# A two-layer SiLU kernel: the order of its first loads, the place of a table load, and a first tile taken in two halves

## The chip, the cores and the metric

The kernel runs on one core of one Trainium2 chip. A core has five engines that work side by side: TensorE (matmuls and transposes), VectorE and ScalarE (elementwise work), GpSimd, and SyncE, which here only issues transfers. ScalarE issues some transfers too. Each of the two has a queue of its own, and both queues are served by the core's 16 DMA engines. The metric is device time in microseconds (us), less is better. Times are the median of several runs; the profile is one execution.

## The reference

x has 2048 rows and 640 columns, w1 is 640 x 1728, w2 is 1728 x 640, all in bf16. The result is `silu(x @ w1) @ w2`, with silu(h) = h * sigmoid(h):

```python
h = jnp.einsum("bsd,df->bsf", x, w1)
h = _silu(h)
out = jnp.einsum("bsf,fd->bsd", h, w2)
```

## The kernel before

**Tiles.** The 640 columns of x, over which the first product is summed, are cut into 5 contraction tiles of 128 (`dt` 0 to 4). The 1728 columns of w1 are 13 tiles of 128 and a half one (`ft`). The 2048 rows are four chunks of 512 (`sc`). The first product is made transposed: a matmul holds a 128 x 128 tile of w1 as its weights and streams 512 columns of x transposed (`xT_sb`) past it, and its result, h transposed, is summed over the five contraction tiles in one of the 8 banks of PSUM (`ps`). ScalarE then takes the sigmoid and VectorE multiplies (lines 197 and 200). The second product (line 319) follows when all of h is there.

**Order.** The program is a list of operations written out by hand: `add` (used throughout) appends an operation with the engine it runs on and the operations it depends on, and each engine runs its own operations strictly in the order of the list, waiting on semaphores where an operation depends on another engine or on a transfer. The order of the calls is thus the order on each engine and in each transfer queue. No planner moves anything.

**The loads at the start.** The first chunk of x comes as it lies in memory (`x0_sb`, helper `load_x0`, line 144) and is transposed by TensorE; the other chunks come through transposing transfers (line 235), which wait for the first of the two late pieces of w1. The transfers of the first chunk are: contraction tile 0 in two halves of rows of 64 KB (`x0_a` on SyncE, `x0_b` on ScalarE), tiles 1 and 2 of 128 KB each (`x0_c`, `x0_d`, ScalarE), and tiles 3 and 4 together, 256 KB (`x0_e`, ScalarE). The first 6 column tiles of w1 come by contraction tile, 192 KB each (`w1_0` to `w1_4`, helper `load_w1`, line 148), all on SyncE; the last two of them wait for `x0_a` and `x0_b`. The other columns of w1 follow in two large pieces. On ScalarE a small sigmoid on a scratch tile (line 155) comes after its four transfers; it has no use but to load the sigmoid's table early (the row ACT_TABLE_LOAD).

**TensorE's start.** TensorE first runs five warm-up matmuls of 512 columns and one of 256 on constants (`warm_up`, line 164). Then it transposes tile 0 of x, four blocks of 128 x 128, into PSUM in two halves, and VectorE copies each half to `xT_sb` (line 178). Two more warm-up matmuls follow, of 512 and 256 columns. Then `column_group` (line 258) runs the first 6 column tiles of w1 for the first chunk: the outer loop goes over the five contraction tiles, the inner one over the 6 column tiles, each with its own bank. The first matmul of each contraction tile waits for that tile of x transposed and for that tile of w1. After the second matmul of a contraction tile, `transpose_next` puts in the four transposes of the next tile of x; VectorE copies the even tiles out (line 178), ScalarE the odd ones (line 180). The remaining column tiles go through `unit` (line 213), all five contraction tiles of one bank in a row.

In what follows, "x's tile n" is contraction tile n of the first chunk of x, and "w1's tile n" is contraction tile n of w1's first six column tiles.

Of the kernel before, what the change touches and what calls it, by code (L numbers as in the profile page):

```python
# [20 lines left out]
class Plan:  # L21
# [9 lines left out]
    def add(self, eng, emit, deps=(), group=None):  # L31
        op = Op(eng, emit, [d for d in deps if d is not None], group)
        self.ops.append(op)
        return op
# [40 lines left out]
def bass_standalone__dense_activation_silu__prompt_kernel(  # L75
# [13 lines left out]
    P = 128  # L89
    H = P // 2  # L90
    SCH = 512
    DT = D // P
# [5 lines left out]
    JB = SCH // P  # L98
# [4 lines left out]
    with ExitStack() as es:  # L103
        def sb(name, shape, dtype):
            return es.enter_context(nc.sbuf_tensor(name, shape, dtype))

        xT_sb = sb("xT_sb", [P, DT, S], bf16)
        w1_sb = sb("w1_sb", [P, DT, F], bf16)
# [9 lines left out]
        ps = es.enter_context(nc.psum_tensor("ps", [P, NBANK, SCH], fp32))  # L118
# [6 lines left out]
        add = plan.add  # L125
        bank_free = [[] for _ in range(NBANK)]
        turn = [0]

        def take_bank():
            b = turn[0] % NBANK  # L130
            turn[0] += 1
            return b


        FA = 6
# [7 lines left out]
        def load_x0(eng, name, j0, j1, d0, d1):  # L143
            return add(eng, lambda e: e.dma_start(
                out=x0_sb[:, j0:j1, d0 * P:d1 * P], in_=x0_v[:, j0:j1, d0 * P:d1 * P]), group=name)

        def load_w1(eng, name, d0, d1, f0, f1, deps=()):
            return add(eng, lambda e: e.dma_start(
                out=w1_sb[:, d0:d1, f0:f1], in_=w1_v[:, d0:d1, f0:f1]), deps, group=name)

        x0_a = [load_x0("sp", "x0_a", 0, JB // 2, 0, 1), load_x0("act", "x0_b", JB // 2, JB, 0, 1)]
        w1_lo = [load_w1("sp", "w1_0", 0, 1, 0, FA * P)]
        x0_c = [load_x0("act", "x0_c", 0, JB, 1, 2), load_x0("act", "x0_d", 0, JB, 2, 3), load_x0("act", "x0_e", 0, JB, 3, DT)]
        w1_lo += [load_w1("sp", f"w1_{dt}", dt, dt + 1, 0, FA * P) for dt in (1, 2)]
        add("act", lambda e: e.activation(out=warm_sb[:, :], in_=warm_sb[:, :], func=ACT.Sigmoid), [warm])  # L155
        w1_lo += [load_w1("sp", f"w1_{dt}", dt, dt + 1, 0, FA * P, x0_a) for dt in (3, 4)]
        w1_dma = [load_w1("sp", f"w1_{name}", 0, DT, w1_cuts[g] * P, min(w1_cuts[g + 1] * P, F))
                  for g, name in enumerate("ab")]
# [3 lines left out]
        def warm_up(columns):  # L162
            for n in columns:
                add("pe", lambda e, n=n: e.matmul(  # L164
                    ps[:, NBANK - 1, 0:n], lhsT=ones[:, 0:P], rhs=ones[:, 0:n], start=True, stop=True))
# [3 lines left out]
        def transpose_x0(dt, j0, j1, b):  # L169

            dst = ps[:, b, :].bitcast(bf16)[:, j0 * P:j1 * P]
            out = xT_sb[:, dt, j0 * P:j1 * P]
            for j in range(j0, j1):
                t = add("pe", lambda e, j=j: e.transpose(  # L174
                    dst[:, (j - j0) * P:(j - j0 + 1) * P], x0_sb[:, j, dt * P:(dt + 1) * P], ident[:, :]),
                    [x0_a[j // (JB // 2)], id_b] if dt == 0 else [x0_c[min(dt, 3) - 1]] + bank_free[b])
            if dt % 2 == 0:
                c = add("dve", lambda e: e.tensor_copy(out=out, in_=dst), [t])  # L178
            else:
                c = add("act", lambda e: e.copy(out=out, in_=dst), [t])  # L180
            bank_free[b] = [c]
            return c

        def x_deps(sc, c0, n):
            return x0T if sc == 0 else x1_of if sc == 1 else [x_dma[sc]]

        def w1_deps(ft):
            return [w1_dma[max(g for g in range(len(w1_dma)) if w1_cuts[g] <= ft)]] if ft >= FA else w1_lo
# [5 lines left out]
        def silu(b, parts, n, pe):  # L194
            s = sig_turn[0] % NSIG
            sig_turn[0] += 1
            a = add("act", lambda e: e.activation(  # L197
                out=sig_sb[:, s, 0:n], in_=ps[:, b, 0:n], func=ACT.Sigmoid), [pe, sig_free[s]])
            for rows, ft, cols in parts:
                v = add("dve", lambda e, rows=rows, ft=ft, cols=cols: e.tensor_tensor(  # L200
                    out=hT_sb[rows, ft, cols], in0=ps[rows, b, 0:n], in1=sig_sb[rows, s, 0:n],
                    op=ALU.mult), [a])
                chunk_done[cols.start // SCH] = v
                if ft == FR:
                    tail_done[cols.start // SCH] = v
            bank_free[b] = [v]
            sig_free[s] = v

        def unit(sc, ft, c0, n):
            b = take_bank()  # L210
            cols = slice(sc * SCH + c0, sc * SCH + c0 + n)
            for dt in range(DT):
                pe = add("pe", lambda e, dt=dt: e.matmul(  # L213
                    ps[:, b, 0:n], lhsT=w1_sb[:, dt, ft * P:(ft + 1) * P], rhs=xT_sb[:, dt, cols],
                    start=(dt == 0), stop=(dt == DT - 1)),
                    x_deps(sc, c0, n) + w1_deps(ft) + bank_free[b] if dt == 0 else ())
            silu(b, [(slice(0, P), ft, cols)], n, pe)

        def tail_unit(sc):
            b = take_bank()  # L220
            for dt in range(DT):
                for hh in range(2):
                    pe = add("pe", lambda e, dt=dt, hh=hh: e.matmul(  # L223
                        ps[hh * H:(hh + 1) * H, b, :], lhsT=w1_sb[:, dt, FR * P:F],
                        rhs=xT_sb[:, dt, (sc + hh) * SCH:(sc + hh + 1) * SCH],
                        start=(dt == 0), stop=(dt == DT - 1), skip_group_check=True),
                        x_deps(sc, 0, SCH) + x_deps(sc + 1, 0, SCH) + w1_deps(FR) + bank_free[b]
                        if dt == 0 else ())
            silu(b, [(slice(hh * H, (hh + 1) * H), FR, slice((sc + hh) * SCH, (sc + hh + 1) * SCH))
                     for hh in range(2)], SCH, pe)  # L230

        x_dma, x1_of, w2_dma = {}, [], []
        for sc in range(1, NSC):
# [7 lines left out]
            if sc == 2:  # L241
                half = FR // 2
# [6 lines left out]

        def column_group(sc, x_dep, w1_dep, between=None):  # L250

            banks = [take_bank() for _ in range(FA)]
            for dt in range(DT):
                for ft in range(FA):
                    deps = bank_free[banks[ft]] if dt == 0 else []
                    if ft == 0:
                        deps = deps + [x_dep[dt], w1_dep[dt]]
                    pe = add("pe", lambda e, dt=dt, ft=ft: e.matmul(  # L258
                        ps[:, banks[ft], :], lhsT=w1_sb[:, dt, ft * P:(ft + 1) * P],
                        rhs=xT_sb[:, dt, sc * SCH:(sc + 1) * SCH],  # L260
                        start=(dt == 0), stop=(dt == DT - 1)), deps)
                    if dt == DT - 1:
                        silu(banks[ft], [(slice(0, P), ft, slice(sc * SCH, (sc + 1) * SCH))], SCH, pe)
                    if between and ft == 1:
                        between(dt + 1)

        def transpose_next(dt):
            if dt < DT:
                x0T.append(transpose_x0(dt, 0, JB, FA + dt % 2))

        half = [transpose_x0(0, k * JB // 2, (k + 1) * JB // 2, FA - 2 + k) for k in range(2)]
        x0T = [half[1]]
        warm_up([SCH, 2 * P])
        column_group(0, x0T, w1_lo, transpose_next)
        for ft in range(FA, FR):
            unit(0, ft, 0, SCH)

        for sc in range(1, NSC):
            if sc == 1:
                column_group(sc, x1_of, w1_lo)  # L280
            for ft in range(FA if sc == 1 else 0, FR):
                unit(sc, ft, 0, SCH)
        reg_done = dict(chunk_done)
# [111 lines left out]
```

## Time and profile before

| what | value |
|---|---|
| median of 3 runs | 126.33 us (125.98 to 126.65) |
| the profiled execution | 126.5 us, its span 125.2 us |
| TensorE busy | 122.1 us, 98% of the span |
| first instruction of TensorE | at 0.77 us |
| first matmul of the column group (L258) | at 4.37 us |
| first matmul of `unit` (L213) | at 12.36 us |
| ACT_TABLE_LOAD (L155) | 1283 ns, from 2.91 us |

The span runs from the first to the last instruction; the execution's own time holds 1.3 us more. In the views, L258 is a line of the kernel before. A group of instructions stands as start, duration, engine, line, operation, the tile written and the tiles read, and how often. PE is TensorE's matmul, PEld its weight load, DVE is VectorE, ACT ScalarE, SPq and ACTq the transfer queues of SyncE and ScalarE. The chain is the sequence of work that ended last, followed back from the end of the execution; "issue" in it is time in which an engine waited for nothing that the profile shows. In the table of stretches each row has the stretch, its length, the busy time of PE, PEld, DVE, ACT and POOL (with the number of instructions that begin), the granted clock, the busy share of the DMA engines and GB/s. A transfer's row ends with its size in KB and the time from its issue to the landing of its last part.

### The profile page before, as it was taken

To read this page: it belongs to the slowest core of one execution; us is meant where nothing else is said; L and a number is where in the kernel's file an instruction comes from. 1 tells how busy PE (TensorE), PEld (TensorE's weight loads), DVE (VectorE), ACT (ScalarE), POOL (GpSimd) and SP (SyncE) were. 2 spreads that over 40 slices of the span, in tenths; PEclk is the share of its full clock that TensorE was granted. 3 is DMA by queue.
4 is the path that set the end of the run, shared out by engine and by line. 5 is a ranking of instruction groups with operands and counts; after the bars stand their busy time and mean duration, and the time that the engine had idled before them with its cause. 6 is when DMAs were issued, how large, how long until landed. Compare 5 with 4: busy or idle time off the path is not lost.

```text
span 125.2 us, 2101 instructions
## 1 busy us (share of the span) xinstructions
PE 122.1 (98%) x902; PEld 57.4 (46%) x902; DVE 45.6 (36%) x72; ACT 39.4 (32%) x69; POOL 0.7 (1%) x6
## 2 busy tenths in 40 slices
PE   7999999999999999999999999999999999999992
PEld 2544444444444444444444444444444444445481
DVE  0112986069766666666673020202020120202022
ACT  0523953087555555555540010101010110101021
POOL 2000000000000000000000000000000000000000
PEclk9999999999999999999999999999999999999999
DMA  3995355589910000000000001114120200112424
GB/s 77 314 385 181 86 113 72 112 237 390 276 43 0 5 0 0 3 0 0 0 0 5 0 0 31 26 22 168 52 105 5 105 0 21 26 21 73 157 98 117
DMA packets 19625, 10.41 MB, mean 83 GB/s; under 512 B 13344, under 2 KB 19616, under 8 KB 19616
## 3 DMA queue, kind: packets, MB, share of 16 engines
q1 hardware_dynamic: 17472, 9.56, 26.6%
q10 hardware_dynamic: 2144, 0.72, 2.2%
q8 instruction: 7, 0.11, 0.4%
q14 instruction: 2, 0.02, 0.1%
HBM read 5.16 MB, written 2.62 MB: 62 GB/s over the span
## 4 chain that ended last, share of the span: by engine, by line
PE 98%; DVE 0%; issue 0%
PE ps L319 47%; PE ps L213 34%; PE ps L258 11%; PE ps L164 3%; PE ps L223 2%; PE ps L174 1%; DVE o_sb L330 0%
## 5 line engine op out<-in xcount | busy, mean ns | idle before, releaser
L319 PE MATMUL ps<-w_sb,hT_sb 64*128 64x512 bf16 (+2 forms) x486 | 47.3, 352 | 0.0
L200 DVE TENSOR_TENSOR hT_sb<-ps,sig_sb 128x512 bf16<-128x512 f32 (+1 forms) x56 | 37.0, 688 | 19.0 <-ACT sig_sb L197 18.9
L213 PE MATMUL ps<-xT_sb,w_sb 128*128 128x512 bf16 x200 | 43.5, 379 | 0.0
L197 ACT ACTIVATE sig_sb<-ps 128x512 bf16<-128x512 f32 x54 | 30.7, 606 | 24.9 <-PE ps L213 16.4
L319 PEld LDWEIGHTS ps<-w_sb,hT_sb 64*128 64x128 bf16 x486 | 23.3, 94 | 23.7
L213 PEld LDWEIGHTS ps<-xT_sb,w_sb 128*128 128x128 bf16 x200 | 19.6, 98 | 23.6
L330 DVE CAST o_sb<-ps 128x512 bf16<-128x512 f32 (+2 forms) x9 | 5.7, 632 | 37.6 <-PE ps L319 37.6
L332 ACT CAST o_sb<-ps 128x512 bf16<-128x512 f32 (+2 forms) x9 | 4.8, 538 | 38.6 <-PE ps L319 38.6
L258 PE MATMUL ps<-xT_sb,w_sb 128*128 128x512 bf16 x60 | 14.4, 387 | 0.0
L319 PE MATMUL ps<-hT_sb,w_sb 64*128 64x512 bf16 x108 | 12.3, 376 | 0.0
L258 PEld LDWEIGHTS ps<-xT_sb,w_sb 128*128 128x128 bf16 x60 | 5.6, 99 | 6.7 <-DVE xT_sb L178 0.7
L319 PEld LDWEIGHTS ps<-hT_sb,w_sb 64*128 64x128 bf16 x108 | 5.2, 94 | 6.6 <-issue 0.4
L330 DVE CAST oT_sb<-ps 128x512 bf16<-128x512 f32 x2 | 1.4, 692 | 11.7 <-PE ps L319 11.7
L332 ACT CAST oT_sb<-ps 128x512 bf16<-128x512 f32 x2 | 1.2, 586 | 13.6 <-PE ps L319 13.6
L178 DVE COPY xT_sb<-ps 128x256 bf16<-128x256 bf16 (+1 forms) x4 | 1.4, 358 | 8.6 <-PE ps L174 8.6
L164 PE MATMUL ps<-const-bfloat16-1.0 128*128 128x512 bf16 (+1 forms) x8 | 3.3, 572 | 0.8 <-PEq L380 0.8
L174 PEld LDWEIGHTS ps<-ident,x_sb 128*128 128x128 bf16 x20 | 1.9, 115 | 1.7 <-DMA x_sb<-in_x_dram 0.7
L174 PE MATMUL ps<-ident,x_sb 128*128 128x128 bf16 x20 | 2.4, 256 | 0.0
L180 ACT COPY xT_sb<-ps 128x512 bf16<-128x512 bf16 x2 | 1.2, 585 | 3.9 <-PE ps L174 3.9
L223 PE MATMUL ps<-xT_sb,w_sb 128*64 128x512 bf16 x20 | 2.3, 381 | 0.0
L155 ACT ACT_TABLE_LOAD x1 | 1.3, 1283 | 2.9 <-issue 2.9
L164 PEld LDWEIGHTS ps<-const-bfloat16-1.0 128*128 128x128 bf16 x8 | 1.0, 137 | 1.9 <-issue 1.9
(9 smaller groups left out, 2.3 us busy)
## 6 DMA issues: line engine op xcount, KB each, us to landing
out_dram<-o_sb SPq DMA_DIRECT2D x14, 160.0 KB, 1.9
w_sb<-in_w_dram SPq DMA_DIRECT2D x1, 1120.0 KB, 7.6
w_sb<-in_w_dram SPq DMA_DIRECT2D x5, 192.0 KB, 4.8
w_sb<-in_w_dram SPq DMA_DIRECT2D x1, 960.0 KB, 5.3
w_sb<-in_w_dram SPq DMA_DIRECT2D x1, 640.0 KB, 6.3
w_sb<-in_w_dram SPq DMA_DIRECT2D x1, 560.0 KB, 7.3
x_sb<-in_x_dram ACTq DMA_DIRECT2D x2, 128.0 KB, 3.8
x_sb<-in_x_dram ACTq DMA_DIRECT2D x1, 256.0 KB, 5.8
```

The source lines that it names most:

```text
L155: add("act", lambda e: e.activation(out=warm_sb[:, :], in_=warm_sb[:, :], func=ACT.Sigmoid), [warm])
L164: add("pe", lambda e, n=n: e.matmul(ps[:, NBANK - 1, 0:n], lhsT=ones[:, 0:P], rhs=ones[:, 0:n], start=True, stop=True))
L174: t = add("pe", lambda e, j=j: e.transpose(dst[:, (j - j0) * P:(j - j0 + 1) * P], x0_sb[:, j, dt * P:(dt + 1) * P], ident[:, :]), [x0_a[j ...
L178: c = add("dve", lambda e: e.tensor_copy(out=out, in_=dst), [t])
L197: a = add("act", lambda e: e.activation(out=sig_sb[:, s, 0:n], in_=ps[:, b, 0:n], func=ACT.Sigmoid), [pe, sig_free[s]])
L200: v = add("dve", lambda e, rows=rows, ft=ft, cols=cols: e.tensor_tensor(out=hT_sb[rows, ft, cols], in0=ps[rows, b, 0:n], in1=sig_sb[rows, ...
L213: pe = add("pe", lambda e, dt=dt: e.matmul(ps[:, b, 0:n], lhsT=w1_sb[:, dt, ft * P:(ft + 1) * P], rhs=xT_sb[:, dt, cols], start=(dt == 0), ...
L223: pe = add("pe", lambda e, dt=dt, hh=hh: e.matmul(ps[hh * H:(hh + 1) * H, b, :], lhsT=w1_sb[:, dt, FR * P:F], rhs=xT_sb[:, dt, (sc + hh) * ...
L258: pe = add("pe", lambda e, dt=dt, ft=ft: e.matmul(ps[:, banks[ft], :], lhsT=w1_sb[:, dt, ft * P:(ft + 1) * P], rhs=xT_sb[:, dt, sc * SCH:( ...
L319: pe = add("pe", lambda e, b=b, n=n, lhsT=lhsT, rhs=rhs, ft=ft: e.matmul(ps[:, b, 0:n], lhsT=lhsT, rhs=rhs, start=(swap == 0 and ft == 0), ...
L330: ev = add("dve", lambda e, b=b, n=n, dst=dst: e.tensor_copy(out=dst, in_=ps[:, b, 0:n]), [pe])
L332: ev = add("act", lambda e, b=b, n=n, dst=dst: e.copy(out=dst, in_=ps[:, b, 0:n]), [pe])
```

## The change

Three things are done.

1. In the list of transfers, x's tiles 1 and 2 go from ScalarE's queue to SyncE's, directly behind w1's tile 0. SyncE's order becomes: half of x's tile 0, w1's tile 0, x's tiles 1 and 2, w1's tile 2, then w1's tiles 3 and 4 and the rest as before.
2. ScalarE's order becomes: the other half of x's tile 0, the table load with the small sigmoid, w1's tile 1 (which was SyncE's), and x's tiles 3 and 4.
3. `column_group` can take a contraction tile in parts of rows. For the first chunk's tile 0 it has two: the first 256 rows of x for all 6 column tiles, then the other 256, so 12 matmuls of 256 columns in place of 6 of 512. The first of each part waits only for that half's copy. The next tile's transposes come after the fourth of these matmuls. The other tiles, and the second chunk's group, have one part as before. The warm-up matmul of 512 columns after the first transposes is taken out; the one of 256 stays.

```diff
         x0_a = [load_x0("sp", "x0_a", 0, JB // 2, 0, 1), load_x0("act", "x0_b", JB // 2, JB, 0, 1)]
         w1_lo = [load_w1("sp", "w1_0", 0, 1, 0, FA * P)]
-        x0_c = [load_x0("act", "x0_c", 0, JB, 1, 2), load_x0("act", "x0_d", 0, JB, 2, 3), load_x0("act", "x0_e", 0, JB, 3, DT)]
-        w1_lo += [load_w1("sp", f"w1_{dt}", dt, dt + 1, 0, FA * P) for dt in (1, 2)]
+        x0_c = [load_x0("sp", "x0_c", 0, JB, 1, 2), load_x0("sp", "x0_d", 0, JB, 2, 3)]
         add("act", lambda e: e.activation(out=warm_sb[:, :], in_=warm_sb[:, :], func=ACT.Sigmoid), [warm])
+        w1_lo += [load_w1("act", "w1_1", 1, 2, 0, FA * P), load_w1("sp", "w1_2", 2, 3, 0, FA * P)]
+        x0_c += [load_x0("act", "x0_e", 0, JB, 3, DT)]
...
-            return x0T if sc == 0 else x1_of if sc == 1 else [x_dma[sc]]
+            return x0T[-1] if sc == 0 else x1_of if sc == 1 else [x_dma[sc]]
...
             banks = [take_bank() for _ in range(FA)]
             for dt in range(DT):
-                for ft in range(FA):
-                    deps = bank_free[banks[ft]] if dt == 0 else []
-                    if ft == 0:
-                        deps = deps + [x_dep[dt], w1_dep[dt]]
-                    pe = add("pe", lambda e, dt=dt, ft=ft: e.matmul(
-                        ps[:, banks[ft], :], lhsT=w1_sb[:, dt, ft * P:(ft + 1) * P],
-                        rhs=xT_sb[:, dt, sc * SCH:(sc + 1) * SCH],
-                        start=(dt == 0), stop=(dt == DT - 1)), deps)
-                    if dt == DT - 1:
-                        silu(banks[ft], [(slice(0, P), ft, slice(sc * SCH, (sc + 1) * SCH))], SCH, pe)
-                    if between and ft == 1:
-                        between(dt + 1)
+                parts = len(x_dep[dt])
+                for h in range(parts):
+                    c0, c1 = h * (SCH // parts), (h + 1) * (SCH // parts)
+                    for ft in range(FA):
+                        deps = [x_dep[dt][h], w1_dep[dt]] if ft == 0 else []
+                        if dt == 0 and h == 0:
+                            deps = deps + bank_free[banks[ft]]
+                        pe = add("pe", lambda e, dt=dt, ft=ft, h=h, c0=c0, c1=c1: e.matmul(
+                            ps[:, banks[ft], c0:c1], lhsT=w1_sb[:, dt, ft * P:(ft + 1) * P],
+                            rhs=xT_sb[:, dt, sc * SCH + c0:sc * SCH + c1],
+                            start=(dt == 0 and h == 0), stop=(dt == DT - 1), skip_group_check=True), deps)
+                        if dt == DT - 1:
+                            silu(banks[ft], [(slice(0, P), ft, slice(sc * SCH, (sc + 1) * SCH))], SCH, pe)
+                        if between and h == 0 and ft == 2 * parts - 1:
+                            between(dt + 1)
...
-                x0T.append(transpose_x0(dt, 0, JB, FA + dt % 2))
+                x0T.append([transpose_x0(dt, 0, JB, FA + dt % 2)])
...
-        x0T = [half[1]]
-        warm_up([SCH, 2 * P])
+        x0T = [half]
+        warm_up([2 * P])
...
-                column_group(sc, x1_of, w1_lo)
+                column_group(sc, [[d] for d in x1_of], w1_lo)
```

In the changed kernel the lines after the loads stand a little lower: the column group's matmul is L264, the transposes L175, the warm-ups L165, `unit` L214.

## The prediction

> **What bounds the kernel now.** I read the page first, for the chain that ended last.
>
> ```profile
> PE 98%; DVE 0%; issue 0%
> PE ps L319 47%; PE ps L213 34%; PE ps L258 11%; PE ps L164 3%; PE ps L223 2%; PE ps L174 1%; DVE o_sb L330 0%
> ```
>
> TensorE is the whole chain, and the last line says where a change of the loading order can act at all: in the warm-up matmuls (L164), the transposes (L174) and the first column group (L258). From L213 on nothing is touched, and TensorE never stands there. So I read the start of the chain in order of time, which has one break: "issue" ahead of 4.37 us, the first real matmul.
>
> ```profile
> 3.28 0.43 PE ps L174 x4
> 3.70 0.64 PE ps L164 x2
> 4.34 0.03 issue
> 4.37 1.01 PE ps L258 x2
> 5.38 0.43 PE ps L174 x4
> 5.80 1.30 PE ps L258 x6
> ```
>
> What ends that break? The timeline names VectorE, but the same timeline shows its two copies done at 3.53 + 0.51 = 4.04.
>
> ```profile
> 3.53 0.51 DVE L178 COPY xT_sb<-ps 128x256 bf16<-128x256 bf16 x2 [2.63 <-PE ps L174]
> 4.34 0.14 PEld L258 LDWEIGHTS ps<-xT_sb,w_sb 128*128 128x128 bf16 x2 [0.69 <-DVE xT_sb L178]
> ```
>
> The wait is for two things, and the other is w1's tile 0. The DMA view around its issue (1.25 us) gives the time to its landing:
>
> ```profile
> w_sb<-in_w_dram SPq DMA_DIRECT2D x1, 192.0 KB, 3.0
> x_sb<-in_x_dram ACTq DMA_DIRECT2D x1, 128.0 KB, 3.3
> ```
>
> So w1's tile 0 lands at 1.25 + 3.0 = 4.25, and the matmul follows 0.12 us later, at 4.37. The second row is x's tile 1, issued by ScalarE at almost the same instant (1.26). The table of stretches shows that the two compete: the DMA engines are full from 2 us on.
>
> ```profile
> 2.00:3.00 1.00, 1.00 (x4) 0.33 (x3) 0.00 (x0) 0.09 (x1) 0.00 (x0) 1.00 0.99 203
> 3.00:4.00 1.00, 1.00 (x8) 0.64 (x6) 0.47 (x2) 1.00 (x1) 0.00 (x0) 1.00 1.08 282
> 4.00:5.00 1.00, 0.97 (x4) 0.28 (x3) 0.03 (x1) 0.42 (x2) 0.00 (x0) 1.00 1.05 297
> ```
>
> The last two columns are the DMA share and GB/s. After the first matmul every tile comes before its turn: the tightest is x's tiles 3 and 4, issued at 2.35, landing 5.8 us later at 8.15, with the transposes that read them at 8.46 right behind the matmul before them.
>
> **The pace of TensorE.** Weight loads of the first 512-column warm-ups start 0.43 us apart (1.15, 1.58, 2.01, 2.43), while ten L258 matmuls from 10.37 take 2.16 us, 0.216 each. The matmul starting at 5.60 still takes 0.43 us by itself, those after 5.86 take 0.38, and early ones 0.63: the pace doubles at about 5.70, 4.93 us after the first matmul at 0.77. The page's granted clock does not show it (9 in every slice). So a start moved from 4.37 to 4.37 - d wins not d but d x (1 - 0.216/0.427) = 0.495 d, as long as the doubling stays at 5.70: the time won is spent at half pace.
>
> **The change, part by part.**
>
> *x's tiles 1 and 2 move from ScalarE's queue to SyncE's, behind w1's tile 0.* w1's tile 0 keeps its place (third issue of all, at 1.25) but loses its competitor. Bounds for its landing: 4.25, as now; or what the bytes ahead of it need if it is served alone. x's two first halves and w1's tile 0 are 320 KiB, 328 kB. The finer table of stretches moved 8 kB up to 2.0, 187 GB/s to 2.5, 219 GB/s to 3.0 and 277 GB/s to 3.5: 211 kB by 3.0, the other 117 kB by 3.42. From the last byte to landing: the two half tiles (131 kB) are through at 2.64 by the same count and land at 0.75 + 2.3 = 3.05, so 0.41; w1's tile 0 lands at 3.83. I take this end, since its nearest row, the two half tiles with nothing behind them, is that situation. TensorE starts 0.12 later: about 3.96, d = 0.41.
>
> *The first contraction tile by halves of rows; the 512-column warm-up goes.* TensorE now ends its warm-ups at 4.14 (transposes to 3.50, then 768 columns at half pace); without the 512 it is free at 3.71. The first matmul needs only the first copy, done at 3.53 + 0.29 = 3.82, not 4.04. So neither holds 3.96, and without these two parts the start would be 4.14. The price: 12 matmuls of 256 columns for 6 of 512, the same columns. Six run at half pace, 0.213 each; six at full pace, where 256 columns are half of 0.216, and weight loads (97 ns) hide behind them as they do now behind 128-column transposes that start 0.056 apart. A price per matmul could be 0 to 0.05 (the transposes'); I take 0, because the transposes carry twice as many loads per column without a gap. That is 0 to 0.3 us in the range. The transposes of tile 1 come after four half matmuls, as many columns as now after two.
>
> *What the moved transfers then meet.* From 3.96: four half matmuls to 4.81, transposes to 5.24, two halves to 5.67, six at full pace to 6.33, tile 1. SyncE's issues are about 0.5 apart, so x's tile 1 goes at 1.75 and tile 2 at 2.25. Tile 1 is due at 4.81. By bytes (459 kB: 350 by 3.5, the rest at 287 GB/s) it is through at 3.88 and lands at 4.29; if it took the time of w1's tile 1, issued at 1.75 now (3.4 us), 5.15, and TensorE would stand 0.46 at half pace, 0.23 us of the end. I take 4.29, by its place in the queue. w1's tile 2 leaves 0.57 later than now (2.78) and at its present 4.8 us lands at 7.6, ahead of 7.8. SyncE's next issues wait for the two half tiles until 3.1, as now, so w1's tiles 3 and 4, the rest of w1 and the transposing loads of x keep their times within 0.1; the first of those lands long ahead of its use at 19.9.
>
> *ScalarE's table load ahead of its next transfers.* ScalarE's own issue ends at 1.23. Load 1.28 and activation 0.23 then end at 2.79; w1's tile 1 goes at 2.80 and x's tiles 3 and 4 at 3.33, 1.05 and 0.98 later than now. Behind the load stand only these two transfers and the copy of tile 1, which moves with its transposes from 5.84 to 5.48 and is long clear; it ends at 6.07, ahead of 6.33. w1's tile 1 at its present 3.4 us lands at 6.20, and the matmul at 6.32 is due at 6.33: no loss. If the transfer is issued beside the load, at 1.3, it is earlier and takes turns with x's tile 1, which is the 0.23 just priced. For x's tiles 3 and 4 the bounds are 8.15, as now, if the bytes ahead of them decide, and 9.13, if the issue does. They take 5.8 us to land now where the first half takes 2.2, so most of it is waiting behind the same bytes, which do not change in sum; I take 8.15. Due at 8.26, it just fits.
>
> [...]
>
> **Sum.** 0.41 x 0.495 = 0.20 us off. On the profiled execution, span 125.2 with 1.3 around it, 126.5 becomes 126.3; it stands 0.17 above the median, so on the median of 126.33 I forecast **126.13**. Half a per cent, 0.63 us, is about what a measurement of this kernel can tell from no change.
>
> **The rivals.**
> 1. *w1's tile 0 lands no earlier.* The DMA engines stay full, and x's tile 1 comes straight behind it from SyncE's queue. Then TensorE waits from 3.71 to 4.37: 126.33. For it: the share of 1.0 from 2 us on. Against: what competes with it now would stand behind it.
>    [...]
> 2. *Slower: x's tiles 3 and 4 become the wait.* If they land 0.98 later, as they are issued, that is 9.13, the transposes start at 9.25 instead of 8.26, at full pace: 0.99 lost, 0.20 won, 127.12. It decides from a landing at 8.34, only 0.19 later than now. For it: no slack. Against: 5.8 us from issue to landing is mostly queueing. A landing in between gives 126.2 to 126.9.
> 3. *The pace doubles later.* The idle time before the first matmul grows from 0.23 to 0.25, or to 0.66 with rival 1. If an idle stretch made the 4.93 us start anew at 3.96, the doubling came at 8.89, 3.19 x 0.495 = 1.58 later: 127.7. Against: the gap of 0.23 now did no such thing.
>    [...]
> 4. *The pace doubles earlier by chance*, or the runs fall as those of before do (125.98 to 126.65): 125.6.
>
> **Chances.** Forecast 0.45 (its own range 125.9 to 126.35), rival 1 0.28, rival 2 in part 0.10 and in full 0.08, rival 3 0.04, rival 4 0.05. The range 125.7 to 126.9 leaves out rival 3, rival 4 and most of rival 2 in full, under 0.2. Faster by over 0.5%: rival 4 and a low tail of the forecast, 0.09. Slower by over 0.5%: rivals 2 in full and 3, 0.12. Within: 0.79.
>
> **What would show it.** In the chain, the first L264 matmul (now L258) at 3.9 to 4.0; at 4.37, rival 1 holds. Its first halves 0.21 apart, the second 0.11. No break ahead of the transposes near 4.8, 6.7 and 8.3; a DMA wait on x at 8.3 is rival 2. Matmuls of 0.63 us still there after 5.7 are rival 3. The forecast is wrong if the column group after the first starts later than now (19.9).

## The result, and the profile after

The changed kernel takes 128.04 us (median of 6 runs, 126.63 to 128.39) against 126.18 (6 runs, 125.96 to 126.93) on the same chip: 1.0108 times as long, interval 1.0074 to 1.0143. It is slower by over half a per cent, and above the range that was forecast. The single times say more than the median: two runs are at 126.63 and 126.97, four at 127.96 to 128.39, and none between. A ratio in this document leaves out runs more than 1.5% above the fastest of the same kernel (none here), so the runs above 127.9 us are also counted one by one.

The profiled execution took 127.96 us, 1.46 more than the one before; its span of 126.6 is 1.4 longer. First the page of the changed kernel, the chain by engine and by line:

```profile
PE 94%; DMA 3%; issue 0%; SPq 0%; DVE 0%
PE ps L325 46%; PE ps L214 34%; PE ps L264 11%; DMA w_sb<-in_w_dram 3%; PE ps L224 2%; PE ps L175 1%; SPq L144 0%; DVE o_sb L336 0%
```

A transfer of w1 has come into a chain that was TensorE alone; the warm-ups (L165) have gone from it, because they no longer reach to the first real matmul. Then the start of the chain in order of time (start, duration, what):

```profile
1.25 3.26 DMA w_sb<-in_w_dram
4.51 0.14 issue
4.64 1.01 PE ps L264 x4
5.65 0.47 PE ps L175 x4
6.12 2.42 PE ps L264 x10
8.54 0.22 PE ps L175 x4
8.76 1.29 PE ps L264 x6
```

Two things are to be seen. The first real matmul starts at 4.64, later than before (4.37), not at 3.96: w1's tile 0 lands at 4.51. And the groups of four transposes are a stop-watch for TensorE's pace: a group takes 0.43 at half pace (0.47 here, with 0.06 in it in which TensorE stands) and 0.22 at full pace. Before, the group at 7.11 took 0.22 already; here only the one at 8.54 does. The doubling is found from the matmuls between, in TensorE's timeline:

```profile
5.91 2.62 PE L264 MATMUL ps<-xT_sb,w_sb 128*128 128x256 bf16 x10
8.37 0.39 PE L175 MATMUL ps<-ident,x_sb 128*128 128x128 bf16 x4
```

Eight matmuls of 256 columns at half pace (0.213) from 5.91 end at 7.61, one of 512 (0.427) at 8.04, and the next ends at 8.37: 0.33, about half way between 0.427 and 0.216. So the pace doubles at about 8.26, against 5.70 before.

**Where the time went.** A doubling 2.56 later costs 2.56 x (1 - 0.216/0.427) = 1.27 us. The first real matmul 0.27 later and the 0.06 of standing, both at half pace, cost 0.33 x 0.216/0.427 = 0.17. Together 1.44, of 1.46 measured. Nothing is lost elsewhere.

**Why w1's tile 0 came late.** ScalarE's timeline shows it:

```profile
0.74 0.51 ACTq L144 DMA_DIRECT2D x_sb<-in_x_dram  x1
1.27 1.28 ACT L154 ACT_TABLE_LOAD   x1 [1.27 <-PEq L386]
1.34 0.42 ACTq L148 DMA_DIRECT2D w_sb<-in_w_dram  x1
1.79 0.46 ACTq L144 DMA_DIRECT2D x_sb<-in_x_dram  x1
```

The table load holds ScalarE for 1.28 us, but not its queue: w1's tile 1 is issued at 1.34, while the load runs, 0.09 after w1's tile 0. In place of x's tile 1, w1's tile 1 is now the competitor, with 192 KB instead of 128. The DMA view of the moved transfers:

```profile
w_sb<-in_w_dram ACTq DMA_DIRECT2D x1, 192.0 KB, 3.4
x_sb<-in_x_dram SPq DMA_DIRECT2D x1, 128.0 KB, 3.7
```

The second row is x's tile 1, issued at 1.75: it lands at 5.45, against 1.26 + 3.3 = 4.56 before. The table of stretches has TensorE's busy time (third column) and the DMA engines, nearly as full as before (shares of 1.07, 0.87 and 1.12 against 0.99, 1.08 and 1.05):

```profile
2.00:3.00 1.00, 1.00 (x4) 0.34 (x3) 0.00 (x0) 0.79 (x2) 0.00 (x0) 1.00 1.07 170
3.00:4.00 1.00, 0.92 (x7) 0.51 (x5) 0.47 (x2) 0.00 (x0) 0.00 (x0) 1.00 0.87 296
4.00:5.00 1.00, 0.36 (x2) 0.28 (x3) 0.04 (x1) 0.00 (x0) 0.00 (x0) 1.00 1.12 306
```

The table counts the last warm-up until its modelled end, 3.92. Its 256 columns, begun at 3.50, have streamed after 0.21 more, at 3.71; counted like this, as everywhere below, TensorE is idle for 0.93 us, against 0.23 before.

**Theories.** Guesses of the author, for the experiments to tell apart. A: with too much idle time in TensorE's first microseconds (0.93 us here, 0.23 before) the pace stays low for one more stretch, and the doubling comes later by it (at 8.26 here, at 5.70 before). B: the moved transfers cost the time, and the doubling fell late by chance. C: half-size matmuls raise the pace later.

### The profile page after: what moved, and what is told of

Its sections match the earlier page's. It is cut to its first block, busy times and chain, and to the rows that moved or that the text cites. A ratio compares the mean times of both kernels' runs of the same rounds, so it can differ in the third digit from the quotient of the medians.

```text
span 126.6 us, 2106 instructions
## 1 busy us (share of the span) xinstructions
PE 122.6 (97%) x902; PEld 58.3 (46%) x907; DVE 45.6 (36%) x72; ACT 39.4 (31%) x69; POOL 0.7 (1%) x6
## 4 chain that ended last, share of the span: by engine, by line
PE 94%; DMA 3%; issue 0%; SPq 0%; DVE 0%
PE ps L325 46%; PE ps L214 34%; PE ps L264 11%; DMA w_sb<-in_w_dram 3%; PE ps L224 2%; PE ps L175 1%; SPq L144 0%; DVE o_sb L336 0%
## 5 line engine op out<-in xcount | busy, mean ns | idle before, releaser
L214 PE MATMUL ps<-xT_sb,w_sb 128*128 128x512 bf16 x197 | 43.3, 379 | 0.2
L214 PEld LDWEIGHTS ps<-xT_sb,w_sb 128*128 128x128 bf16 x200 | 19.6, 98 | 23.6
L264 PE MATMUL ps<-xT_sb,w_sb 128*128 128x512 bf16 (+1 forms) x64 | 15.2, 392 | 0.8 <-DMA w_sb<-in_w_dram 0.7
L264 PEld LDWEIGHTS ps<-xT_sb,w_sb 128*128 128x128 bf16 x66 | 6.8, 107 | 7.2 <-DVE xT_sb L179 1.1
L165 PE MATMUL ps<-const-bfloat16-1.0 128*128 128x512 bf16 (+1 forms) x7 | 2.9, 563 | 0.8 <-PEq L386 0.8
L175 PEld LDWEIGHTS ps<-ident,x_sb 128*128 128x128 bf16 x20 | 1.8, 112 | 1.7 <-DMA x_sb<-in_x_dram 0.7
L175 PE MATMUL ps<-ident,x_sb 128*128 128x128 bf16 x20 | 2.4, 255 | 0.0
L165 PEld LDWEIGHTS ps<-const-bfloat16-1.0 128*128 128x128 bf16 x7 | 0.9, 135 | 1.9 <-issue 1.9
L154 ACT ACT_TABLE_LOAD x1 | 1.3, 1283 | 1.3 <-PEq L386 1.3
```

Of the source, the lines that this page charges most:

```text
L165: add("pe", lambda e, n=n: e.matmul(ps[:, NBANK - 1, 0:n], lhsT=ones[:, 0:P], rhs=ones[:, 0:n], start=True, stop=True))
L175: t = add("pe", lambda e, j=j: e.transpose(dst[:, (j - j0) * P:(j - j0 + 1) * P], x0_sb[:, j, dt * P:(dt + 1) * P], ident[:, :]), [x0_a[j ...
L214: pe = add("pe", lambda e, dt=dt: e.matmul(ps[:, b, 0:n], lhsT=w1_sb[:, dt, ft * P:(ft + 1) * P], rhs=xT_sb[:, dt, cols], start=(dt == 0), ...
L264: pe = add("pe", lambda e, dt=dt, ft=ft, h=h, c0=c0, c1=c1: e.matmul(ps[:, banks[ft], c0:c1], lhsT=w1_sb[:, dt, ft * P:(ft + 1) * P], rhs= ...
```

## The experiments

Each kernel ran 12 times (one 6 times), with 23 to 35 runs of the kernel before on the same chip. Of each kernel one run was profiled, so whether a run above 127.9 had a late doubling is known only where it is the profiled one. Of all 128 runs of the kernel before, one is there (128.36); the others end at 127.25.

**1. The idle time filled.** The changed kernel with 1024 columns of warm-up more.

```diff
-        warm_up([2 * P])
+        warm_up([SCH, SCH, 2 * P])
```

> The changed kernel with 1024 columns of warm-up more after the first transposes, so that TensorE is busy until about 4.57 us instead of 3.71. Theory A (the idle stretch ahead of the first real matmul, 0.93 us in the changed kernel's profile, keeps TensorE at half pace for one more stretch): the pace doubles at 5.7 or so as before, not at 8.3, the slow group of runs near 128 goes, and the median is 126.2 to 126.6. Theory B (the reordered transfers cost the time, and the doubling falls by chance): the first real matmul still comes at 4.6 and the median stays near 128.0. Theory C (half-size matmuls do not raise the pace): stays near 128.0 too.

126.81 against 126.56, ratio 1.0040 (1.0016 to 1.0065); 0 of 12 above 127.9. Its chain:

```profile
3.71 1.07 PE ps L165 x3
4.77 0.85 PE ps L264 x4
5.62 0.43 PE ps L175 x4
6.05 1.34 PE ps L264 x10
7.39 0.22 PE ps L175 x4
```

The same ten matmuls take 1.34 instead of 2.42, although the first real matmul starts no earlier than 4.57. The upper group is gone: A holds, B and C do not. The median is 0.2 above A's range; what stays, 0.4%, is not explained by A.

**2. The idle time made in the kernel before.**

```diff
-        warm_up([SCH, 2 * P])
+        warm_up([2 * P])
```

> The kernel before without the 512-column warm-up after the first transposes, nothing else: TensorE is free at 3.71 and stands until w1's tile 0 lands, 4.25, so 0.66 us idle in place of 0.23. Theory A: the pace doubles later, near 8.3, in most runs and the median is 127.3 to 128. Theory B: no transfer is moved, so 126.2. Theory C: no half-size matmul, so 126.2.

126.34 against 126.56, ratio 0.9992 (0.9966 to 1.0017) without 2 of 12 at 128.17 and 128.23. A's numbers fail for most runs. The profile says why: w1's tile 0 landed early in this execution, and TensorE stood 0.38 us, not 0.66.

```profile
3.50 0.42 PE L164 MATMUL ps<-const-bfloat16-1.0 128*128 128x256 bf16 x1
4.09 0.72 PE L258 MATMUL ps<-xT_sb,w_sb 128*128 128x512 bf16 x2 [0.17 <-DVE xT_sb L178]
```

The pace is full already in the second of the two matmuls from 4.09. So both the landing and the doubling move from run to run. If A holds, idle time raises the odds of a late doubling and does not make it certain.

**3. The transfers alone.** The kernel before with the new order of the loads (the lines of the change's first hunk).

> The kernel before with the new order of transfers and the early table load alone; warm-ups and the whole first tile as before. TensorE is free at 4.14, w1's tile 0 lands at 4.5 as in the changed kernel, so some 0.45 us idle. Theory A: between, with a doubling that is late in part of the runs: 126.4 to 127.5. Theory B: all of the loss, 127.8 to 128.1. Theory C: 126.3 to 126.5, only the 0.27 later start at half pace.

126.90 against 126.56, ratio 1.0037 (1.0009 to 1.0064) without one of 12 at 128.72; another is at 127.62. As A expected; B expected all of the loss.

**4. The halves alone.** The kernel before with the new `column_group`; loads and warm-ups as before.

> The kernel before with the first tile in halves of rows, transfers and warm-ups as before (0.23 us idle). Theory A: 126.2, as before. Theory B: 126.2. Theory C: 127.5 to 128.1, with the pace doubling near 8.3.

126.48 against 126.56, ratio 0.9999 (0.9971 to 1.0026), 0 of 12. Halves cost and win nothing. C is out. The profile holds a comparison that nobody planned: w1's tile 0 landed at 4.50 and the first real matmul started at 4.64, as late as in the changed kernel's profile. But the 512-column warm-up left only 0.50 us idle, the pace doubled at 5.29, and the run took 126.52. In this run a late first matmul alone did not bring the late doubling.

**5. The 512-column warm-up kept.** The changed kernel with `warm_up([SCH, 2 * P])`.

> The changed kernel with the 512-column warm-up kept, nothing else: TensorE is free at 4.14 instead of 3.71 and so stands 0.1 to 0.5 us instead of 0.5 to 0.9. Theory A (a stretch of idle time of some 0.7 us or more keeps the pace low for one more period; less does not): at most 2 of 12 runs near 128, median 126.6 to 127.0, as with the two fillers. Rival A' (any idle time delays the doubling in proportion): the median falls half way, 127.2 to 127.6, without two groups. Rival B (the transfers): 128.

126.97 against 126.42, ratio 1.0038 (1.0020 to 1.0057); 0 of 12 above 127.2. In the profile TensorE stands 0.30 us ahead of the first real matmul and 0.40 ahead of the next transposes, and still doubles at 6.2. A holds, a delay in proportion to the idle time (A') does not.

**6. No warm-ups after the first transposes, in the kernel before.**

```diff
-        warm_up([SCH, 2 * P])
```

> The kernel before without both warm-ups after the first transposes: transfers as before, TensorE free at 3.50, so 0.5 to 1.1 us idle, about as much as in the changed kernel. Theory A: two groups, with a third or more of the runs at 127.5 to 128.5. Rival A': one group, 126.5 to 127.2. Rival B: 126.4, no transfer being moved.

126.56 against 126.42, ratio 0.9985 (0.9961 to 1.0010) without 4 of 12 at 127.90 to 128.20: two groups, with no transfer moved. B is out as the only cause of an upper group. The other eight are at 125.86 to 126.83, no slower than before.

**7. Filled, and w1's tile 1 held back.** Experiment 1 with the transfer that ScalarE issues waiting for x's first halves.

```diff
-        w1_lo += [load_w1("act", "w1_1", 1, 2, 0, FA * P), ...
+        w1_lo += [load_w1("act", "w1_1", 1, 2, 0, FA * P, x0_a), ...
```

> The changed kernel with 1024 columns of warm-up more and, besides, w1's tile 1 on ScalarE's queue held back until x's two first halves have landed, about 3.1 us, so that it no longer runs beside w1's tile 0 and x's tile 1. Theory: what is left of the loss with the fillers (0.4%) is x's tile 1 landing at 5.3 to 5.5 instead of 4.6 to 5.2, because w1's tile 1 is issued beside the table load and competes with it; then x's tile 1 lands at 4.3 to 4.7 here and the median falls from 126.8 to 126.5 or less. Rival: the fillers themselves cost it, by holding the first real matmul at 4.57; then it stays at 126.8.

127.85 (6 runs, 127.22 to 128.28, 3 of them above 127.9) against 126.42, ratio 1.0105 (1.0072 to 1.0139): both expectations miss. w1's tile 0 lands at 1.25 + 2.6 = 3.85, x's tile 1 at 1.75 + 2.6 = 4.35, as the theory said. But the transfers held back become the wait:

```profile
3.08 4.27 DMA w_sb<-in_w_dram
7.35 0.14 issue
7.48 0.59 PE ps L264 x2
```

w1's tile 1, issued at 3.08, lands at 7.35 and holds TensorE at full pace; x's tiles 3 and 4, issued at 3.45, take 5.7 us, to 9.15. The profiled run is at 127.56 and doubles its pace at 6.5; none of the three runs above 127.9 was profiled. This kernel comes near to what the prediction took the change for, a queue that waits behind the table load (until 3.08 here, 2.80 there).

**8. w1's tile 0 first in SyncE's queue.** The changed tile and warm-ups; otherwise the loads of before, with x's half behind w1's tile 0.

```diff
-        x0_a = [load_x0("sp", "x0_a", 0, JB // 2, 0, 1), load_x0("act", "x0_b", JB // 2, JB, 0, 1)]
-        w1_lo = [load_w1("sp", "w1_0", 0, 1, 0, FA * P)]
+        x0_b = load_x0("act", "x0_a", 0, JB // 2, 0, 1)
+        w1_lo = [load_w1("sp", "w1_0", 0, 1, 0, FA * P)]
+        x0_a = [x0_b, load_x0("sp", "x0_b", JB // 2, JB, 0, 1)]
...
```

> The changed kernel's tile in halves, with w1's tile 0 as SyncE's first transfer, x's two first halves one behind the other (ScalarE's first and SyncE's second), and the other transfers and the table load as in the kernel before; the 512-column warm-up stays out. If w1's tile 0 is late because of its place in the queue, it lands at 3.5 or so, TensorE's first real matmul comes at 3.8 to 4.0 without a long idle stretch, and the median is 126.0 to 126.3. If landing depends little on the place, the idle stretch stays and part of the runs are near 128.

126.89 against 126.42, ratio 1.0047 (1.0020 to 1.0074), one of 12 at 128.51. Neither expectation: in the profile x's half lands at 3.55 instead of 2.9, the transposes start at 3.60, and the first real matmul comes at 4.38, no earlier than before: the wait has only changed its owner. The loss of this run, 127.24, is the doubling once more. TensorE stood 0.53 us ahead of the transposes, and the pace doubled at 7.15, 1.45 later than in the profile before. That makes 1.45 x 0.494 = 0.72, of 0.74 measured. Whether this idle time moved the doubling, or whether it fell later by chance, one profile can't tell.

**9. The changed kernel again.**

> The changed kernel itself again, 12 runs on one chip beside the next three. Theory A (a stretch with some 0.9 us of idle time in it does not count as busy, so the pace doubles a stretch later): two groups, near 126.6 to 127.0 and near 128 to 128.4, with about half or more of the runs in the upper one. If the first six runs were a bad draw, fewer than a fifth are in it.

127.62 against 126.50; six runs at 126.58 to 127.24 and six at 127.99 to 128.81. The ratio, 1.0059 (1.0019 to 1.0099), is without the four highest. With the first six runs, 10 of 18 are in the upper group, as A expected. This time the profiled run is one of the lower group, 126.67:

```profile
3.50 0.42 PE L165 MATMUL ps<-const-bfloat16-1.0 128*128 128x256 bf16 x1
4.56 0.81 PE L264 MATMUL ps<-xT_sb,w_sb 128*128 128x256 bf16 x4 [0.64 <-DMA w_sb<-in_w_dram]
```

TensorE stood 0.85 us, hardly less than the 0.93 of the first profile. But the four matmuls take 0.81 instead of 1.01, because the pace doubles among them, at about 5.04. So the same kernel, with nearly the same idle time, falls on either side.

**10. The change without its transfers.** Halves, 512-column warm-up out, loads and table load of before.

> The change without its reordering of transfers: first tile in halves, 512-column warm-up out, loads and table load as in the kernel before. TensorE is free at 3.71, as in the changed kernel. Theory A: a lower group as in the kernel before without the 512 columns (125.8 to 126.6) and an upper one near 128 of one to four runs of 12. Rival B (the reordered transfers are needed for the loss): no run over 127.3.

126.45 against 126.50, ratio 0.9998 (0.9973 to 1.0024), 0 of 12: fewer than A expected, and what its rival B expected. In its profile w1's tile 0 landed at 1.27 + 2.7 = 3.97 and TensorE stood 0.4 us. Taking the warm-up out alone is mostly harmless (2 of 24 runs in experiments 2 and 10); together with the moved loads, which land later, it is not.

**11. Idle time where nothing real waits.** The kernel before with three warm-ups at the start instead of six.

```diff
-        warm_up([SCH] * 5 + [2 * P])
+        warm_up([SCH] * 3)
```

> The kernel before with three warm-up matmuls at the start instead of six, so that TensorE stands from 2.05 to about 3.05 us, ahead of the transposes, where it would have nothing real to do; everything else as before. No transfer and no real matmul moves. Theory A (idle time counts wherever it lies in the stretch): the doubling comes later, from 5.5 to 8.9 us, and the median rises to 127.0 to 127.6 with runs up to 128.2. Rival A'' (only the stand right ahead of the real matmuls matters): 126.4.

127.14 against 126.50, ratio 1.0066 (1.0034 to 1.0099) without one run at 129.46; three of 12 above 127.9. No transfer has moved, and the first real matmul starts at 4.43, 0.06 later than before. The profiled run is one of those three, 128.21:

```profile
4.43 1.01 PE ps L258 x2
5.44 0.43 PE ps L174 x4
5.86 2.56 PE ps L258 x6
8.42 0.43 PE ps L174 x4
8.85 1.48 PE ps L258 x6
10.32 0.22 PE ps L174 x4
```

The stop-watch reads 0.43 still at 8.42, and six matmuls take 2.56 instead of 1.30. In this run TensorE stood 0.93 us ahead of the transposes, which by itself delays nothing, and 0.45 ahead of the first real matmul, and the pace doubles at about 9.1, 3.4 later than in the profile before. That makes 3.4 x 0.494 = 1.68, of 1.71 by which the run is slower. Experiment 2 had only the second of these two waits (0.38), and its median did not rise. Experiment 11 is the cleanest evidence for A.

**12. The small gap of the kernel before filled.** `warm_up([SCH, SCH])` after the transposes.

> The kernel before with 256 columns of warm-up more after the first transposes (512 and 512), so that TensorE is busy until 4.35 us. Theory A: no run near 128, median 126.3 to 126.5, as before, since 0.23 idle is tolerated anyway and the first real matmul hardly moves.

126.64 against 126.50, ratio 1.0016 (0.9993 to 1.0038), 0 of 12. As expected, with the median 0.1 above the range; nothing is won.

**13. The table load ahead, alone.** The kernel before with ScalarE's small sigmoid ahead of x's tiles 1 to 4.

> The kernel before with one part of the change alone: ScalarE's table load and small sigmoid ahead of its transfers of x's tiles 1 to 4; queues, tiles and warm-ups as before. Theory (transfers are issued beside the table load, as the changed kernel's trace shows): ScalarE's next transfer is issued at about 1.35 instead of 1.26, nothing lands more than 0.2 later, and the median is that of before, 126.4 to 126.5. Rival (the table load holds the queue): x's tile 1 is issued at 2.8 and lands after 5.5, and the median rises by 0.5 or more.

126.66 against 126.56, ratio 1.0000 (0.9976 to 1.0024), 0 of 12. Again the transfers go out beside the load, at 1.34:

```profile
1.27 1.28 ACT L153 ACT_TABLE_LOAD   x1 [1.27 <-PEq L380]
1.34 1.54 ACTq L144 DMA_DIRECT2D x_sb<-in_x_dram  x3
```

The time is that of before: this part of the change costs nothing that these runs can tell. One landing misses the expectation: x's tile 1 comes at 1.34 + 4.0 = 5.34, 0.8 later than in the profile before, though other profiles with the order of before have it as late as 5.26 (experiment 6).

**14. All early tiles in SyncE's queue, in the order of their use.** The changed kernel's tile and warm-ups; ScalarE keeps only x's tiles 3 and 4, held back to 3.1.

```diff
...
+        x0_c = [load_x0("sp", "x0_c", 0, JB, 1, 2)]
+        w1_lo += [load_w1("sp", "w1_1", 1, 2, 0, FA * P)]
+        x0_c += [load_x0("sp", "x0_d", 0, JB, 2, 3)]
+        w1_lo += [load_w1("sp", "w1_2", 2, 3, 0, FA * P)]
...
```

> The changed kernel (halves, 512-column warm-up out, table load early) with all of w1's and x's early tiles in SyncE's queue in the order of their use and x's tiles 3 and 4 alone on ScalarE, held back until x's two first halves have landed, about 3.1 us. Theory (the competing transfer on ScalarE's queue made w1's tile 0 and x's tile 1 late): w1's tile 0 lands at 3.8 to 4.0 and x's tile 1 at 4.2 to 4.5, TensorE's first real matmul comes at about 4.0 with 0.3 us idle, no run is near 128, and the median is 126.0 to 126.4, unless x's tiles 3 and 4 land after 8.2. Rival (the move to one queue itself costs): the landings stay at 4.3 and 5.3 and the lower group at 126.6 or more.

127.34 against 126.56, ratio 1.0059 (1.0029 to 1.0089), with 2 of 12 at 128.18 and 128.21 where the theory had none. w1's tile 0 lands as the theory had it, at 1.26 + 2.6 = 3.86, and the first real matmul starts at 4.02; x's tile 1, at 1.76 + 3.0 = 4.76, misses its 4.2 to 4.5. The time misses too. One thing the profile shows is that SyncE's queue issues one transfer per 0.5 us here (at 1.26, 1.76, 2.23 and 2.78):

```profile
2.23 0.51 SPq L148
2.73 0.04 issue
2.78 4.40 DMA x_sb<-in_x_dram
7.18 0.05 issue
7.22 0.40 PE ps L178 x4
```

x's tile 2 goes out at 2.78, a full 1 us later than in the kernel before, lands at 7.18 and is waited for, 0.39 us at full pace. The profiled run, 126.76, is one of the faster; what the slower ones lost beside this is not shown.

## Why the prediction was wrong, point by point

- *What bounds the kernel, and the wait for w1's tile 0 behind the view's "VectorE":* right; the view of the changed kernel names the transfer itself.
- *w1's tile 0 lands at 3.83, first real matmul at 3.96, x's tile 1 lands at 4.29:* wrong, 4.51, 4.64 and 5.45. The failed step is "ScalarE's table load ahead of its next transfers ... w1's tile 1 goes at 2.80". It went at 1.34, and the competitor that the step on w1's tile 0 had removed was back. The count of bytes itself was good: with the competitor really gone (experiments 7 and 14) the tile landed at 3.85 and 3.86, and in the five profiles with w1's tile 1 beside it at 4.26 to 4.51. That is not the whole cause, though: with the order of before, where x's tile 1 competes, eight profiles have 3.85 to 4.50, so the prediction's 4.25 was one draw out of a wide range. The prediction had the other issue time, 1.3, as a case, but priced it only for x's tile 1 (0.23 us) and not for w1's tile 0, nor for the idle time that follows.
- *The 512-column warm-up goes at no price, since TensorE would wait anyway:* wrong, and this is the step that made the size of the loss. It was given a cost only as time on the path; what it hid was an idle stretch. Its removal (0.43) and the later landing (0.27) raised the idle time from 0.23 to 0.93, and 10 of 18 runs are in the upper group, whose one profile shows the late doubling. Kept (experiment 5) or made longer (experiment 1), the upper group goes.
- *Rival 3, the pace doubles later:* this is what came, at 8.26 instead of 5.70, with a chance of 0.04. Its argument against, that a gap of 0.23 did no harm, said nothing of a gap three times as long, which the prediction itself put at 0.66 if rival 1 came with it. That its price, 1.58, is near the 1.6 between the groups (126.8 and 128.4 in the middle) is luck, for the count behind it, 4.93 us that start anew at the first real matmul, was wrong: in the changed kernel's profile the doubling came 3.6 us after it, in experiment 3 1.5. In the profiles without the late doubling, the pace doubles anywhere from 4.2 or earlier (experiment 6, where the first two real matmuls, from 4.24, take 0.59 together instead of 1.01) over 5.0 (9), 5.3 (4), 5.7 (before), 6.0 (1), 6.2 (5) and 6.5 (7) to 6.6 (13). The 127 lower runs of the kernel before spread over 125.57 to 127.25; if the doubling makes all of that, it moves, by estimate, over 1.68 / 0.494 = 3.4 us from run to run. Nor does the doubling move in proportion to the idle time: with 0.93 us the changed kernel's profile doubled at 8.26, with 0.85 in experiment 9 at 5.04, and with 0.70 in experiment 5 at 6.2. What sets the moment of the doubling is not shown; the granted clock of the rows, 1.00 throughout, does not show even the doubling. That idle time brings runs into the upper group is shown (10 of 18 in the changed kernel, 4 of 12 in experiment 6, 3 of 12 in experiment 11), and that an upper run doubles late in the two profiled ones (8.26 in the result's, 9.1 in experiment 11's); by what it does so is open.
- *Half matmuls for free:* right (ratios of 0.9999 and 0.9998 in experiments 4 and 10).
- *The early table load hides:* right in its effect (a ratio of 1.0000 in experiment 13), by another reason than given: it did not hold the next transfer up, which went out at 1.34, 0.07 after the load's start.
- *Load 1.28 and activation 0.23 end at 2.79:* right, 2.80; the activation follows the load at once in the changed kernel (at 2.57, after 1.27 + 1.28 = 2.55) as in the one before (at 4.20, after 2.91 + 1.28 = 4.19).
- *Rival 2, x's tiles 3 and 4 land as late as they are issued:* not in the changed kernel, where they were issued earlier, at 1.79. But where their issue was really late (3.45 in experiment 7) they landed 5.7 us after it, at 9.15, as that rival's price had it, and w1's tile 1, held back in the same way, took 4.27 us where the prediction counted 3.4. Nor does the issue alone decide: in experiment 14 the same two tiles, issued at 3.09, landed 4.4 us later, at 7.5, before the 8.15 of the prediction. Neither of its two bounds held in all of these profiles.
- *A start moved by d wins 0.495 d:* the factor should have been 0.216/0.427 = 0.506; it made no difference, the two being nearly one half each.
- *What stays open.* With the idle time filled or the warm-up kept, the moved transfers still cost 0.4% (experiments 1, 3, 5), and nothing of it is there without them (4, 10). In the five profiles with the new order and w1's tile 1 early, x's tile 1 lands at 5.3 to 5.6; in those with the old order at 4.5 to 5.4. That fits a later start wherever the pace doubles early (TensorE stands 0.35 us for it at full pace in experiment 9's profile), but the two runs without the competitor made other transfers late, so its share is argued and not shown. Which landings and doublings the runs without a profile had is open for every kernel here. That no version beat the kernel before is a result of these trials, not a proof.

## What to carry to other kernels

Dummy work that "only fills a wait" can have a second job: ask what its engine's pace needs before taking it out (without the 512 columns 10 of 18 runs of the changed kernel were in the upper group, with them 0 of 12), and look at single runs, since the loss showed here as two groups, 1.6 us apart, and not as a shift. When a transfer is put behind another instruction in an engine's list, ask whether the queue is held by the engine's work at all; here a table load of 1.28 us did not hold it (issue at 1.34), a wait on a semaphore did (3.08). And a transfer's issue time is a resource of its own: where 0.5 us pass per issue, as in experiment 14, moving a tile to the other queue moves what stands behind it (x's tile 2 to 2.78, 1 us later than in the kernel before).

## What the runs showed that was not expected

- A table load of 1283 ns did not hold the transfers behind it on ScalarE: in six profiles the next was issued 0.06 to 0.07 us after the load's start (1.34 after 1.27).
- Idle time of 0.93 us ahead of the transposes, with the first real matmul only 0.06 us later, cost 0.66% (experiment 11).
- The same transfer in the same place landed at 3.85 to 4.5 us from one execution to the next (w1's tile 0 with the old order of loads), 0.65 us of spread that no reordering here removed without a price.
